# Six chunks, the first weights and the first block in a computed order; a norm with two matmuls; a tile-wise end

## The chip, the cores and the metric

One core of one Trainium2 chip. The metric is the device time of one execution in microseconds (us). TensorE (PE) multiplies, VectorE (DVE) does elementwise work, ScalarE (ACT) activations and copies, GpSimd (POOL) and SyncE (SP) issue DMAs. Every engine runs its own instructions in order, and waits on semaphores of the others.

## The reference

A gated linear recurrence over 768 steps in 32 heads, and then two gated MLPs with weights of their own, the second behind an RMS norm:

```
for t in range(S):                                   # S = 768, head_dim D = 48
    state = alpha[:, :, t, :, None] * state + outer(k[:, :, t], v[:, :, t])
    y[:, :, t] = q[:, :, t] @ state
x  = y, as [B * S, H * D]                            # 3072 tokens x 384
x  = (silu(x @ w_gate) * (x @ w_val)) @ w_out        # d_ff = 1536
xn = x / sqrt(mean(x * x) + 1e-6) * rms_g
out = (silu(xn @ w_gate2) * (xn @ w_val2)) @ w_out2
```

## The kernel before

The recurrence is cut into 24 chunks of 128 steps (6 for each of 4 batches, batch by batch in turn), 8 heads at a time as four pairs. Within a chunk it goes by levels b = 1, 2, 4, ... 64. `start_chunk` multiplies q by alpha (DVE). `products` (DVE) multiplies neighbouring alphas, `merge` (DVE) multiplies them into q and k in place, and `copy_qk` (ACT) copies q and k of a level out before the next merge overwrites them. `scores` (PE) multiplies the copies, `masks` (DVE) and `copies_p` (ACT) bring the scores out of PSUM, and `outputs` (PE) multiplies them with v into the tile Y. `kv` and `state` carry the state on, `turn` of k (L479) is a transpose that `kv` needs, and `split_x` (ACT, then DVE) brings Y out as x, in a high and a low part. The first six chunks start from level 1 and take the diagonal on DVE (`direct_ops`); the later ones start from level 4, with a longer `direct_ops`.

The MLPs run over blocks of 3 or 4 chunks (seven in the first layer, six in the second). Each block goes over 12 slices f of d_ff: three (block 0) or nine matmuls into g, the same into v, `s = silu(g) * v` (ACT, DVE), and an output group `o` one f later. Block 0 of the first layer, written (0,0), uses the weights in plain fp32 as `conv` has put them together from raw words (ACT and DVE; tiles `room` and `x`); the other blocks use weights split into a high and a low part (`split_hi`, `split_lo`) and x so split too, which takes three matmuls for one.

The order of the instructions is the order in which the program is written out. `chunk(n, T)` issues what chunk n does in slot T, and a chunk begins every 12 slots (NS). `run` first issues the 44 slots up to `UNTIL[0]`, with a step of `conv` every fifth slot (PRE); these hold chunks 0 to 2 and the first slots of chunk 3. Then it goes over the MLP's points (three for each f), and after each of them issues a share of the slots that belong to the block: chunks 3 to 5 and the first eight slots of chunk 6 beside block (0,0), chunks 6 to 8 beside (0,1), and so on. Weight loads go out on POOL's queue, all others on SP's. vl, vn and dir (v by level, v, and the operands of `direct_ops`) have one buffer, qk and its alpha two.

The second layer needs the norm of each block, `norm_steps`, issued step by step beside the block before. It sums squares over partitions with four matmuls that have one column each (L571), works on columns of 4, and spreads the result with four matmuls of 128 columns (L590). The last three output tiles go out through `evac`: copy (ACT) into one of two tiles `ev`, and a store from SP.

## Time and profile before

| | us |
|---|---|
| median of 3 runs (1121.33 to 1121.57) | 1121.56 |
| the profiled execution | 1124.23 |
| its span, first to last instruction | 1122.5 |
| PE busy in the span | 1066.4 (95%) |
| DVE busy | 655.1 (58%) |
| ACT busy | 415.8 (37%) |

The profile is of one execution. A matmul in plain fp32 shows as two records there (x6 for three matmuls). Busy times are sums of instruction durations, and instructions that follow each other closely overlap a little. A name on the left of an arrow is written, on the right read; L651 is a line of the kernel above. "Idle before" is the time that an engine stood still ahead of an instruction, with what released it.

### The profile page before, as it was taken

To read this page: it belongs to the slowest core of one execution; us is meant where nothing else is said; L and a number is where in the kernel's file an instruction comes from. 1 tells how busy PE (TensorE), PEld (TensorE's weight loads), DVE (VectorE), ACT (ScalarE), POOL (GpSimd) and SP (SyncE) were. 2 spreads that over 40 slices of the span, in tenths; PEclk is the share of its full clock that TensorE was granted. 3 is DMA by queue.
4 is the path that set the end of the run, shared out by engine and by line. 5 is a ranking of instruction groups with operands and counts; after the bars stand their busy time and mean duration, and the time that the engine had idled before them with its cause. 6 is when DMAs were issued, how large, how long until landed. Compare 5 with 4: busy or idle time off the path is not lost.

```text
span 1122.5 us, 25564 instructions
## 1 busy us (share of the span) xinstructions
PE 1066.4 (95%) x10944; PEld 887.4 (79%) x10944; DVE 655.1 (58%) x1361; ACT 415.8 (37%) x770; POOL 45.6 (4%) x81
## 2 busy tenths in 40 slices
PE   2668999999999999999999999999999999999997
PEld 2545669999999878878888888888888888888886
DVE  4779966887778877767737777723323324233221
ACT  3465624543344433333425444331232322322222
POOL 2012000000000000000000000000000000000000
PEclk9889999999999999999999999999999999999999
DMA  8657524443464443444324343010000100100000
GB/s 259 181 175 235 157 80 128 114 119 97 109 152 135 125 135 103 120 122 113 96 81 173 127 141 127 16 41 1 29 29 1 48 10 1 57 1 1 29 1 29
DMA packets 56018, 103.64 MB, mean 92 GB/s; under 512 B 7392, under 2 KB 40672, under 8 KB 55904
## 3 DMA queue, kind: packets, MB, share of 16 engines
q1 hardware_dynamic: 50592, 80.37, 24.7%
q0 software_dynamic: 5312, 21.63, 5.7%
q8 instruction: 86, 1.41, 0.5%
...
## 4 chain that ended last, share of the span: by engine, by line
PE 85%; DVE 2%; DMA 2%; ACT 1%; issue 1%; SPq 0%; ACTq 0%; DVEq 0%; POOLq 0%
PE g L651 25%; PE o L692 25%; PE v L651 25%; PE Y L340 4%; PE Y L297 3%; DMA x2d<-ev 1%; PE Y L380 1%; PE Y L335 1%; PE Y L479 1%; PE Y L590 0%; DMA ydd<-yd 0%; PE Y L571 0%; DVE qk L230 0%; DMA room<-w 0%; ACT ev L612 0%
## 5 line engine op out<-in xcount | busy, mean ns | idle before, releaser
L661 DVE TENSOR_TENSOR s<-s,v 128x512 f32<-128x512 f32 (+1 forms) x156 | 100.6, 645 | 315.4 <-PE v L651 314.5
L651 PE MATMUL g<-xhi,w 128*128 128x512 f32 (+1 forms) x864 | 280.5, 379 | 0.0
L651 PE MATMUL v<-xhi,w 128*128 128x512 f32 (+1 forms) x864 | 280.2, 378 | 0.0
L692 PE MATMUL o<-hh,w 128*128 128x512 f32 (+1 forms) x864 | 208.6, 376 | 0.0
L658 ACT ACTIVATE s<-g 128x512 f32<-128x512 f32 (+1 forms) x156 | 88.0, 564 | 270.6 <-PE g L651 238.9
L667 ACT ACTIVATE hh<-s 128x512 fp32r<-128x512 f32 (+1 forms) x144 | 87.2, 606 | 270.6 <-DVE s L661 270.5
L651 PEld LDWEIGHTS g<-xhi,w 128*128 128x128 f32 x864 | 161.2, 188 | 27.1
L651 PEld LDWEIGHTS v<-xhi,w 128*128 128x128 f32 x864 | 161.2, 188 | 26.1
L692 PEld LDWEIGHTS o<-hh,w 128*128 128x128 f32 x864 | 159.8, 188 | 26.1
L651 PE MATMUL g<-xlo,w 128*128 128x512 f32 (+1 forms) x432 | 163.2, 378 | 2.5 <-DVE xlo L411 2.5
L651 PE MATMUL v<-xlo,w 128*128 128x512 f32 (+1 forms) x432 | 162.4, 376 | 0.0
L692 PE MATMUL o<-hl,w 128*128 128x512 f32 (+1 forms) x432 | 122.0, 389 | 1.7 <-ACT ev L612 1.5
L673 DVE TENSOR_TENSOR hl<-s,hh 128x512 fp32r<-128x512 f32 (+1 forms) x144 | 94.2, 654 | 45.4 <-ACT hh L667 37.2
L651 PEld LDWEIGHTS g<-xlo,w 128*128 128x128 f32 x432 | 81.1, 188 | 17.0 <-DVE xlo L411 4.3
L651 PEld LDWEIGHTS v<-xlo,w 128*128 128x128 f32 x432 | 81.2, 188 | 12.5
L692 PEld LDWEIGHTS o<-hl,w 128*128 128x128 f32 x432 | 76.9, 188 | 17.3 <-ACT ev L612 2.5
L230 DVE TENSOR_TENSOR qk<-qk,bpb 128x512 f32<-128x512 f32 x96 | 65.9, 687 | 25.8 <-PE Y L297 15.3
L253 ACT ACTIVATE kc<-qk 128x512 f32<-128x512 f32 x72 | 45.5, 631 | 47.5 <-DVE qk L230 47.2
L340 PE MATMUL Y<-pt,vl 64*32 64x64 f32 (+1 forms) x2880 | 48.3, 228 | 3.4 <-issue 2.1
L340 PEld LDWEIGHTS Y<-pt,vl 64*32 64x32 f32 (+1 forms) x2880 | 41.3, 110 | 10.7 <-issue 7.5
L230 DVE TENSOR_TENSOR qk<-qk,bpa 128x512 f32<-128x512 f32 x48 | 32.9, 686 | 4.5 <-ACT px L253 2.8
L318 DVE TENSOR_TENSOR pt<-Y,mask 128x256 f32<-128x256 f32 x63 | 23.4, 417 | 15.8 <-ACT pt L329 15.8
...
## 6 DMA issues: line engine op xcount, KB each, us to landing
...
```

Of the source, the lines that this page charges most:

```text
L230: self.nc.vector.tensor_tensor(out=v, in0=v, in1=sub(t, o, [(1, 2), (2, nb), (0, b)]), op=ALU.mult)
L253: self.nc.scalar.activation(out=sub(t, 0, [(NP * 64, 2), (b, NP * 64 // b), (1, b)]), in_=v, func=AF.Copy)
L297: self.nc.tensor.matmul(out=sc[o:o + w, p] if l < 3 else sc[o:o + w, p // 2, p % 2], lhsT=kc[d, p, gs], rhs=qc[d, p, gs], start=True, stop ...
L318: self.nc.vector.tensor_tensor(out=p, in0=sc, in1=m, op=ALU.mult)
L335: self.nc.tensor.matmul(out=self.Y[:, k, 0:C], lhsT=yn[:, C * k:C * k + C], rhs=self.ident, is_transpose=True, start=True, stop=False, ski ...
L340: mm = lambda o, a, x: self.nc.tensor.matmul(out=o, lhsT=a, rhs=x, start=False, stop=False, skip_group_check=True)
L651: nc.tensor.matmul(out=ps[:, :N], lhsT=a, rhs=x, start=(q == 0), stop=(q == len(ops) - 1))
L658: nc.scalar.activation(out=s[:, :N], in_=g[:, :N], func=AF.Silu)
L661: nc.vector.tensor_tensor(out=s[:, :N], in0=s[:, :N], in1=v[:, :N], op=ALU.mult)
L667: nc.scalar.activation(out=hh[:, :N], in_=s[:, :N], func=AF.Copy)
L673: nc.vector.tensor_tensor(out=hl[:, :N], in0=s[:, :N], in1=hh[:, :N], op=ALU.subtract)
L692: nc.tensor.matmul(out=O[gj][i][:, :N], lhsT=a[:, 128 * i:128 * i + 128], rhs=x[:, :N], start=(f == 0 and q == 0), stop=(f == NF - 1 and q ...
```

## The change

Before the second block there are no slots any more. `plan_chunk` (chunks 0 to 5, BEGIN), `plan_weights`, `plan_mlp` (block 0) and `plan_split` hand every step to a list scheduler, `Plan`, with its engine, a duration, what it reads and writes, and a due time. `Plan.order` repeatedly looks, on each engine, at the steps whose inputs are there, takes those that could begin within 0.3 us of the earliest, and of these the one that is due first; the steps are issued by the start times that come out. Odd chunks get second buffers for vl, vn and dir (`vlo`, `vno`, `diro`) in tiles that are free so early. Chunk 0's second half and the zero fill of its tile go out on ACT's queue, a first activation stands ahead of them for its table, and the loads of weights 1 and 2 wait until chunks 0 and 1 have made some copies (`gate`). Block (0,1) now has 44 slots beside it (all of chunk 6 to 8).

The norm squares and adds as before, splits the sum into a high and a low part, and multiplies both with a 128 x 128 matrix of ones, so that every partition gets the sum of every token; the rest goes over 128 x 512 instead of 128 x 4, and the four matmuls of L590 fall away. The last output piece goes tile by tile, high parts first, each tile has a place of its own in SBUF, the third goes in halves, and ACT and DVE share the copies.

```diff
-PRE = 0.2
-CONV1, CONV2 = 1.34, 1.0
+CONV2 = 1.0
+AHEAD, RATE = 0.3, 280.0
+ARRIVE = ((7.0, (("qk", 0), ("al", 0))), (10.0, (("dir", 0),)), (14.0, (("hi", 0), ("lo", 0))))
 EXTRA = 2
+BEGIN = 6
+START, SPAN, PIECE, LEAD = 50.0, 29.0, 7.3, 11.0
...
+class Plan:
+
+
...
+    def add(self, engine, us, fn, reads=(), writes=(), due=0.0, size=0):
+        reads = [t for t in reads if t not in writes]
+        need = set()
+        for t in reads:
+            need |= self.last.get(t, set())
+        for t in writes:
+            need |= self.last.get(t, set()) | self.seen.get(t, set())
...
+    def order(self):
+
+        free, end, got, wire = {}, {}, [], 0.0
+        todo = list(range(len(self.ops)))
+        while todo:
+            ready = {}
+            for i in todo:
+                engine, us, _, need, due, _ = self.ops[i]
+                if all(j in end for j in need):
+                    t = free.get(engine, 0.0)
+                    for j in need:
+                        t = max(t, end[j] + (0.0 if self.ops[j][0] == engine and not self.ops[j][5] else self.sem))
+                    ready.setdefault(engine, []).append((t, due, i))
+            best = None
+            for engine, c in ready.items():
+                first = min(c)[0]
+                pick = min((x for x in c if x[0] <= first + self.ahead), key=lambda x: (x[1], x[0], x[2]))
+                if best is None or pick[0] < best[0]:
+                    best = pick
+            t, _, i = best
+            engine, us, _, _, _, size = self.ops[i]
+            free[engine] = end[i] = t + us
+            if size:
+                wire = max(wire, t + us) + size / self.rate
+                end[i] = wire + 1.8
+            todo.remove(i)
+            got.append((t, i))
+        self.times = got, end
+        return [self.ops[i][2] for _, i in sorted(got)]
...
+    def other(self, n):
+        return n < BEGIN and n % 2
+
+    def vl(self, n, l):
+        return self.vlo[l] if self.other(n) else self.vlt[l]
 
     def load_vn(self, n):
-        t = self.vnt[n] = self.a1.tile([128, NP, 2, D], F32, tag="vn", name="vn")
+        t = self.vnt[n] = self.vno if self.other(n) else self.a1.tile([128, NP, 2, D], F32, tag="vn", name="vn")
...
+    def plan_chunk(self, n):
+
+        add, i, early = self.plan.add, n % 2, self.early(n)
+        qk, al, vn, dr = ("qk", i), ("al", i), ("vn", i), ("dir", i)
+        t0, w = (9 + LEAD * n, 1.3) if early else (START + SPAN * (n - 3), SPAN / 20)
+        due = lambda x: t0 + w * x
+        bp = lambda b: al if b == 1 else ("bp", b, i)
...
+        if n:
+            add("SP", .8, lambda: self.load_qk(n), (), (qk, al), due(-9), 590)
+        if n:
+            add("SP", .4, lambda: self.load_vn(n), (), (vn,), due(-2), 196)
+            add("SP", .8, lambda: (self.load_dir(n, 0), self.load_dir(n, 1)), (), (dr,), due(-3), 393)
...
+        add("DVE", .61, lambda: self.start_chunk(n), (al,), (qk, "bpa", ("bpb", i)), due(0))
+        for l, b in enumerate(LEVELS):
+            if b < 64:
+                add("ACT", .58, lambda l=l: self.copy_qk(n, l), (qk,), (al,) if b == 32 else (("kc", l),), due(l))
+            if b == 1:
+                add("DVE", .35, lambda: self.products(n, 1), (al, "bpa"), (bp(2),), due(.5))
+            if b == 64:
+                break
+            add("DVE", .61, lambda b=b: self.merge(n, b), (bp(b), *bpt(b)), (qk,), due(l + 1))
+            add("DVE", (.21, .14, .1, .09, .08, .08)[l], lambda b=b: self.products(n, 2 * b),
+                (bp(2 * b), *bpt(2 * b), *bpt(4 * b)), (bp(4 * b),), due(l + 1.1))
...
+        if early:
+            for ls in ((0, 1), (2,), (3, 4), (5, 6)):
+                score(ls, due(max(ls)))
+        else:
+            score(tuple(range(NL)), due(7))
+        add("DVE", .61, lambda: self.merge(n, 64), (bp(64), ("bpb", i)), (qk,), due(8.5))
...
+        add("ACT", 1.14, lambda: step(0), (hi,), (w,), due)
+        add("ACT", 1.2, lambda: step(1), (), (lo,), due + .1)
+        add("DVE", .66, lambda: step(2), (), (w,), due + 1)
+        add("DVE", 1.28, lambda: step(3), (lo,), (w,), due + 2)
+        add("DVE", 1.28, lambda: step(4), (hi,), (w,), due + 3)
...
+        add("PE", 1.94, lambda: gv("g", 0), (("W", f), *xs), ("g",), due)
+        add("ACT", .45, silu, ("g",), (s,), 0)
+        add("PE", 1.94, lambda: gv("v", 1), (("W", f), *xs), ("v",), due + 1)
+        add("DVE", .48, mult, ("v",), (s,), 0)
+        if f < NF - 1:
+            add("PE", 1.94, lambda: self.out_piece((0, 0), f, T["s"], self.W32[0, f], self.O), (("W", f), s), ("o0", "o1", "o2"), due + 3)
...
-        ss = self.Y[:, 0, 0:MB]
-        for c in range(MB):
-            nc.tensor.matmul(out=ss[:, c:c + 1], lhsT=q0[:, c * C:(c + 1) * C], rhs=self.ones[:, 0:1], start=True, stop=True,
-                             skip_group_check=True)
-        yield
-        a, r, t = (self.n1.tile([128, MB], F32, tag=t, name=t) for t in ("msq", "rstd", "tmpn"))
+        hl = [self.n1.tile([128, NW], F32R, tag=t, name=t) for t in ("sqh", "sql")]
+        nc.scalar.activation(out=hl[0], in_=q0, func=AF.Copy)
+        yield
+        tt(out=hl[1], in0=q0, in1=hl[0], op=ALU.subtract)
+        yield
+        ss = self.Y[:, 0]
+        for i in range(2):
+            nc.tensor.matmul(out=ss, lhsT=self.ones, rhs=hl[i], start=(i == 0), stop=(i == 1))
+        yield
+        a, r, t = self.n1.tile([128, NW], F32, tag="msq", name="msq"), q0, q1
         nc.vector.tensor_scalar(out=a, in0=ss, scalar1=1.0 / DM, scalar2=EPS, op0=ALU.mult, op1=ALU.add)
+        yield
         nc.vector.tensor_scalar(out=t.bitcast(I32), in0=a.bitcast(I32), scalar1=1, scalar2=None, op0=ALU.logical_shift_right)
         nc.vector.tensor_scalar(out=r.bitcast(I32), in0=t.bitcast(I32), scalar1=-1, scalar2=0x5F3759DF, op0=ALU.mult, op1=ALU.add)
         for _ in range(3):
             yield
             tt(out=t, in0=r, in1=r, op=ALU.mult)
+            yield
             stt(out=t, in0=t, scalar=-0.5, in1=a, op0=ALU.mult, op1=ALU.mult)
+            yield
             stt(out=r, in0=t, scalar=1.5, in1=r, op0=ALU.add, op1=ALU.mult)
-        yield
-        for c in range(MB):
-            nc.vector.tensor_scalar(out=q0[:, c * C:(c + 1) * C], in0=self.ident, scalar1=r[:, c:c + 1], scalar2=None, op0=ALU.mult)
-        yield
-        rb = self.Y[:, 1]
-        for c in range(MB):
-            o = slice(c * C, (c + 1) * C)
-            nc.tensor.matmul(out=rb[:, o], lhsT=self.ones, rhs=q0[:, o], start=True, stop=True, skip_group_check=True)
         yield
...
-                stt(out=x[:, k], in0=x[:, k], scalar=self.g2[:, k:k + 1], in1=rb, op0=ALU.mult, op1=ALU.mult)
+                stt(out=x[:, k], in0=x[:, k], scalar=self.g2[:, k:k + 1], in1=r, op0=ALU.mult, op1=ALU.mult)
...
-    NORM = 13 + KT + 1
+    NORM = 20 + KT + 1
...
+    def last_piece(self, ops, o):
+
+        nc = self.nc
+        N, c0 = MB * C, (NCH - MB) * C
+        cols = [(0, slice(0, N)), (1, slice(0, N)), (2, slice(0, N // 2)), (2, slice(N // 2, N))]
+        t = [self.n1.tile([128, NW], F32, tag=f"sq{i % 2}", name="ev") if i else self.rp.tile([128, NW], F32, tag="ev", name="ev", bufs=2)
+             for i in range(KT)]
+        for i in range(KT):
+            for q, (a, x) in enumerate(ops):
+                nc.tensor.matmul(out=o[i][:, :N], lhsT=a[:, 128 * i:128 * i + 128], rhs=x[:, :N], start=False,
+                                 stop=(q == len(ops) - 1))
+        for n, (i, c) in enumerate(cols):
+            if n % 2:
+                nc.vector.tensor_copy(out=t[i][:, c], in_=o[i][:, c])
+            else:
+                nc.scalar.activation(out=t[i][:, c], in_=o[i][:, c], func=AF.Copy)
+            (nc.scalar if n == 3 else nc.sync).dma_start(
+                out=self.d["out"][128 * i:128 * i + 128, c0 + c.start:c0 + c.stop], in_=t[i][:, c])
...
+        half(nc.sync, 0, 0)
+        half(nc.scalar, 0, 1)
+        pad(nc.scalar, 0, 0)
+        pad(nc.scalar, 0, 1)
+        warm = self.const.tile([128, 1], F32, name="warm")
+        nc.vector.memset(warm, 0.0)
+        nc.scalar.activation(out=warm, in_=warm, func=AF.Silu)
...
+        for n in range(BEGIN):
+            self.plan_chunk(n)
+            if n < 2:
+                held = self.kcx[0][:, 0, 0, 0:1]
+                plan.add("POOL", .2, lambda n=n, a=held: nc.gpsimd.tensor_copy(out=gate[:, n:n + 1], in_=a),
+                         (("kc", 0), ("kc", 3)), ("gate",), 0)
+                plan.add("POOL", 1.6, lambda n=n: self.raw_at(n + 1), ("gate",), (("hi", n + 1), ("lo", n + 1)), 0, 1180)
...
+        for f in range(NF):
+            self.plan_weights(f)
+            self.plan_mlp(f)
+        for f in range(BEGIN):
+            self.plan_split(f)
+        for fn in plan.order():
+            fn()
...
-                    side, total = (self.slot(i) for i in range(UNTIL[j], UNTIL[j + 1])), UNTIL[j + 1] - UNTIL[j]
+                    a = UNTIL[j] if j > 1 else NS * (BEGIN - 1)
+                    side, total = (self.slot(i) for i in range(a, UNTIL[j + 1])), UNTIL[j + 1] - a
```

On DVE, at the end of chunk 0's levels (qk_88 is the tile of even chunks, qk_89 that of odd ones; the last number is the level b). Before:

```order
L222 TENSOR_TENSOR bpb<-bpb 128x4
L318 TENSOR_TENSOR px<-early,mask 128x256 x2
L318 TENSOR_TENSOR pt<-early,mask 128x256
L421 TENSOR_TENSOR dir<-dir 128x384
L318 TENSOR_TENSOR pt<-early,mask 128x256
L431 TENSOR_REDUCE dir<-dir 128x8
L429 TENSOR_TENSOR yn<-vn,dir 128x384
L158 TENSOR_SCALAR x_118<-x_118 128x1152
L318 TENSOR_TENSOR pt<-early,mask 128x256
L230 TENSOR_TENSOR qk_88<-qk_88,bpb 128x2x4x64
L239 TENSOR_TENSOR qk_89<-qk_89 128x512
```

and now:

```order
L273 TENSOR_TENSOR qk_88<-qk_88,bpb 128x2x32x8
L465 TENSOR_TENSOR yn<-vn,dir 128x384
L273 TENSOR_TENSOR qk_88<-qk_88,bpb 128x2x16x16
L357 TENSOR_TENSOR px<-early,mask 128x256 x2
L273 TENSOR_TENSOR qk_88<-qk_88,bpb 128x2x8x32
L280 TENSOR_TENSOR qk_89<-qk_89 128x512
L357 TENSOR_TENSOR pt<-early,mask 128x256 x2
L265 TENSOR_TENSOR bpa<-qk_89 128x256
L273 TENSOR_TENSOR qk_88<-qk_88,bpb 128x2x4x64
L357 TENSOR_TENSOR pt<-early,mask 128x256
L273 TENSOR_TENSOR qk_89<-qk_89 128x2x256
```

The first product of chunk 1 (qk_89) moved ahead of chunk 0's last merge and two of its masks, and chunk 0's own diagonal moved in between its merges.

On PE, at the start of block 0 (x_118 and x_121 hold weights 0 and 1, x_119 and x_122 weights 2 and 3). Before:

```order
L651 MATMUL g<-x_417,x_118 128x384 x3
L651 MATMUL v<-x_417,x_118 128x384 x3
L297 MATMUL Y<-px 32x32 x32
L297 MATMUL Y<-kc 64x64 x24
L297 MATMUL Y<-qk_89 64x64 x16
L651 MATMUL g<-x_417,x_118 128x384 x3
L651 MATMUL v<-x_417,x_118 128x384 x3
L479 MATMUL Y<-ident,qk_89 128x128 x4
L692 MATMUL o_1080<-s,x_118 128x384
L692 MATMUL o_1081<-s,x_118 128x384
```

and now:

```order
L654 MATMUL g<-x_504,x_121 128x384 x3
L654 MATMUL v<-x_504,x_121 128x384 x3
L654 MATMUL g<-x_504,x_121 128x384 x3
L872 MATMUL o_961<-s,x_121 128x384
L872 MATMUL o_962<-s,x_121 128x384
L872 MATMUL o_963<-s,x_121 128x384
L654 MATMUL v<-x_504,x_121 128x384 x3
L654 MATMUL g<-x_504,x_122 128x384 x3
L336 MATMUL Y<-px 32x32 x32
L336 MATMUL Y<-kc 64x64 x24
```

Chunk 3's scores (Y) moved behind the first g of weight 2, and an output group stands two groups behind the v that it depends on.

On PE in the second layer, at the norm. Before, the first of the two places:

```order
L651 MATMUL v<-xhi,w 128x512 x2
L651 MATMUL v<-xlo,w 128x512
L651 MATMUL v<-xhi,w 128x512
L571 MATMUL Y<-ones,sq_8043 128x1 x4
L692 MATMUL o_7999<-hl,w 128x512
```

and now:

```order
L872 MATMUL o_7997<-hh,w 128x512
L872 MATMUL o_7998<-hh,w 128x512
L768 MATMUL Y<-sqh,ones 128x512
L768 MATMUL Y<-sql,ones 128x512
L834 MATMUL g<-xhi,w 128x512
```

The second place (L590, four matmuls) is gone.

## Rows read from the trace of the kernel before

**Rows 1.** The page's busy tenths of 40 equal slices; PEclk is the granted clock.

```profile
PE   2668999999999999999999999999999999999997
...
DVE  4779966887778877767737777723323324233221
...
PEclk9889999999999999999999999999999999999999
```

**Rows 2.** By stretch: length, busy PE, PEld, DVE, ACT, POOL; clock, DMA share, GB/s.

```profile
0.00:69.50 69.50, 31.39 (x1053) 27.36 (x1053) 40.64 (x89) 29.60 (x51) 10.54 (x24) 0.90 0.77 220
69.50:165.80 96.30, 89.98 (x1310) 56.83 (x1311) 82.46 (x138) 53.55 (x83) 11.66 (x21) 0.98 0.51 158
165.80:239.90 74.10, 73.67 (x1112) 69.15 (x1111) 59.07 (x142) 34.18 (x74) 3.91 (x6) 1.00 0.39 112
```

**Rows 3.** DVE's waits up to 69.5: total us, times, longest.

```profile
DVE qk L239 <- DMA qk<-zero: 8.6, 1, 8.6
DVE qk L230 <- ACT px L253: 8.2, 8, 2.3
DVE qk L230 <- ACT kc L253: 4.1, 7, 0.6
DVE dir L421 <- DMA dir<-qn: 2.2, 1, 2.2
...
DVE qk L230 <- ACT qk L253: 1.5, 2, 0.9
```

**Rows 4.** DVE in time order: start us, us, instruction, [idle before].

```profile
9.65 0.69 DVE L239 TENSOR_TENSOR qk<-qk 128x512 f32<-128x512 f32 x1 [8.65 <-DMA qk<-zero]
...
11.69 0.69 DVE L230 TENSOR_TENSOR qk<-qk 128x512 f32<-128x512 f32 x1 [1.01 <-ACT px L253]
...
18.96 0.69 DVE L230 TENSOR_TENSOR qk<-qk,bpb 128x512 f32<-128x512 f32 x1 [0.92 <-ACT qk L253]
...
26.36 0.68 DVE L239 TENSOR_TENSOR qk<-qk 128x512 f32<-128x512 f32 x1
```

**Rows 5.** SP in time order, its first loads.

```profile
0.74 1.79 SPq L94 DMA_DIRECT2D qk<-qka  x4
```

**Rows 6.** Tile qk up to 12 us: its transfers, from issue to landing.

```profile
DMA to landing us min/median/max: 4.1/7.5/9.7
```

**Rows 7.** PE in time order, block 0, and the first matmul of the second.

```profile
69.53 3.90 PE L651 MATMUL g<-x,x 128*128 128x384 f32 x6 [3.96 <-ACT x L405]
...
129.28 2.10 PE L651 MATMUL g<-x,x 128*128 128x384 f32 x6
...
159.31 2.10 PE L651 MATMUL g<-x,x 128*128 128x384 f32 x6
...
165.83 0.63 PE L651 MATMUL g<-xhi,w 128*128 128x384 f32 x1
```

**Rows 8.** PE in time order, around the norm's matmuls of one block.

```profile
690.26 0.95 PE L571 MATMUL Y<-ones,sq 128*128 128x1 f32 x8
691.08 0.94 PE L692 MATMUL o<-hl,w 128*128 128x512 f32 x3
...
713.62 1.06 PE L590 MATMUL Y<-sq,ones 128*128 128x128 f32 x8
714.43 0.48 PE L651 MATMUL v<-xhi,w 128*128 128x512 f32 x1
```

**Rows 9.** The chain that ended last: start us, us; a group of nine.

```profile
598.42 2.04 PE g L651 x9
```

**Rows 10.** PE and ACT in time order, the end of the span.

```profile
1113.90 0.96 PE L692 MATMUL o<-hl,w 128*128 128x512 f32 x3 [0.20 <-DVE hl L673]
...
1114.70 1.53 PE L692 MATMUL o<-hh,w 128*128 128x512 f32 x6
...
1118.55 0.60 ACT L612 ACTIVATE ev<-o 128x512 f32<-128x512 f32 x1 [1.65 <-DMA out<-ev]
```

398 lines of the change are left out of this document (238 added, 160 removed).

## The prediction

> **What bounds the kernel now.** I read the busy tenths first [rows 1]. From about a tenth of the span on, PE stands at 9 in nearly every slice, and its granted clock is full: there the kernel is bound by PE, and only PE work taken out of it, or a wait of PE's, shortens it. The first slices are different. PE is at 2 to 8 and DVE at 4 to 9. So the second view is the busy time by stretch [rows 2], cut at the first matmul of the first block (69.5 us) and at the first of the second block (165.8). Up to 69.5 the three early chunks are made; DVE is busy for 40.64 us of it and idle for 28.9, and PE for less than half. From 69.5 to 165.8 the first block runs; PE is at 90 of 96.3. From 165.8 on PE has no room (73.67 of 74.1).
>
> Why DVE idles early is the third view [rows 3]: 8.6 us for the first load, 2.2 us for a later one, and 8.2 + 4.1 + 1.5 = 13.8 us for ScalarE's copies. The rows of one chunk show how [rows 4]: before each of the six merges of a level DVE waits for the copy of the level before, 1.01 us the first time and 0.92 the last, 4.2 us in sum over the six. Nothing else is there to run, since the next chunk's first product comes only at 26.36, when this chunk is through. The early part is a chain of latencies, one chunk after the other.
>
> **Step 1: when the first block can start.** The change puts the next chunk's product right behind the sixth merge, and gives odd chunks buffers of their own, so that two chunks are under way at once. DVE's work up to the first block hardly changes: by the order, 22 merges instead of 25 stand ahead of it, the rest nearly cancels, so 40.6 - 3 x 0.69 = 38.5 us. The first product now runs at 9.65, released by a zero fill that POOL issued. In the change these fills and half of chunk 0's load go out on ScalarE's queue. The transfers into this tile took 4.1 to 9.7 us to land [rows 6], so the product could run between 4.9 and 9.65; I take 7.0, nearer to the middle, since the fills stand behind the half load. Of the 28.9 us of idle time 9.5 lie ahead of the first product and 19.4 behind it. All of these would stay if the copies hold every chunk up as before, none if the second chunk always has something ready. I keep 5: the 4.2 of the first chunk, which is still alone for its six merges, and a little at the end of chunk 2. That gives 7.0 + 38.5 + 5 = 50.5 for the first matmul of block 0, against 69.53; the ends are 7.0 + 38.5 = 45.5 and 65.
>
> One rule speaks against the 7.0. In the rows the four loads of the tile kept SP's queue for 1.79 us [rows 5], and the fills came from POOL. The Trainium skill (DMA: Bandwidth & Descriptors, section "Issuing engines are not separate DMA queues") says that transfers started by several engines run interleaved on the same 16 DMA engines, so that a second issuing engine saves the issue time alone. By that rule the product would come some 1.3 us earlier, at 8.4, and the sum would be 1091.4 instead of 1090. The spread of 4.1 to 9.7 us for one tile is what I go by; the rule's value lies inside my range.
>
> **Step 2: the first block.** Where nothing waits, four f of block 0 with one chunk take from 129.28 to 159.31, 30.0 us [rows 7]. Twelve f with three chunks are 90.1, less one output group of 2.1 that falls into the next block: 88.0. Now the stage takes 165.83 - 69.53 = 96.3, so 8.3 are lost, 1.8 of them to the half clock at its start (3.90 us for six matmuls, 2.10 later). The planner's order keeps the same groups. DVE's 82.46 us there [rows 2] lose chunk 6's share (11, step 3), and 71 fit beside 88. It leaves some places tight (an output group stands right behind the product that it needs), and PE comes from a sparse stretch as before. I take 4.5: the 1.8 again and 2.7 of waits; the ends are 0 and the 8.3 of now. So the second block starts at 50.5 + 88.0 + 4.5 = 143.0: 22.8 us earlier.
>
> **Step 3: the second block.** The whole of chunk 6 now runs beside block 1, 44 slots instead of 36. These eight slots are DVE and ScalarE work. At 59.07 us for 36 slots [rows 2] they cost at most 13.1; I take 11, since the MLP's own products in the 59 don't grow, and 1 for one more weight split. DVE then has 71 of 74.1 us. PE's work is the same, so this is hidden if the waits of DVE, 15 us now, shrink to 3. PE never stands still for long there, so these are waits of an engine that keeps to PE's pace, and they shrink when it has more to do. I charge 1 us; the ends are 0 and 12.
>
> **Step 4: the norm.** Its matmuls stand in PE's full stretch. The four of one column hold the stream from 690.26 to 691.08, the four of the spread-out row from 713.62 to 714.43: 0.82 + 0.81 us a block [rows 8]. Nine matmuls of 128x512 take 2.04 [rows 9], so the two new ones take 0.45. That is 1.18 a block and 7.1 for six. DVE's part grows from columns of 4 to rows of 512: nine steps at no more than the 0.69 of a product of that size, 6 us a block. This lies beside PE, with DVE at 2 or 3 tenths from two thirds of the span on [rows 1]. If the new operand came late by one DVE instruction (0.69) each time, 4.1 would go; its subtraction stands an output group ahead of its use, so I take 7.1, with 3.0 as the other end.
>
> **Step 5: the end.** Now the third evacuation waits for the first tile's store: it runs at 1118.55 to 1119.15 [rows 10], and the span ends 3.35 later. The last matmul ends at 1114.70 + 1.53 = 1116.23, after a wait of 0.20 for the low part, which is now needed later. With a third tile and halves on two engines the last evacuation ends about 0.4 (two thirds of the 0.60) behind that, at 1116.4, less the 0.2: 1116.2, and the span 3.35 later: 2.9 us less. Ends 2.0 (the fourth store queues) and 3.2 (the half evacuation takes 0.3 and its start gains too).
>
> **Sum.** 22.8 - 1.0 + 7.1 + 2.9 = 31.8. The profiled execution took 1124.23 with a span of 1122.5; it would take 1092.4. The median of the runs lies 2.7 below it, so 1089.8: **1090**.
>
> **Rivals.** First, *the early part stays a chain*. The merges wait for the copies, the copies share ScalarE with the weights' steps, which the new order puts between them, and a plan can't shorten an instruction. Then all 19.4 us stay, the block starts at 65, and the time is 1090 + 14.5 = 1104. For it: 13.8 us of these waits are for ScalarE. Against it: ScalarE is busy for only 29.6 of 69.5 us [rows 2], so the waits are latency, which a second chunk can fill. Chance 0.15.
>
> Second, *DVE becomes the bound beside block 1*: step 3 costs 12 instead of 1, time 1101. For it: 71 of 74.1. Against it: DVE waits there for what comes at PE's pace, and can work ahead of it where it has more to do. Chance 0.10.
>
> Third, on the other side, *loads that come late stop an engine in order*. A chunk's first product needs its load, the load must wait until the buffer's last reader is through, and in the new order this product stands ahead of the last merges of the chunk before: a late load holds up two chunks and the weights behind them. Chunks 2 to 6 have such a load. With 31.8 us to lose, it decides from 6.4 us uncovered at each of the five. At 9.7, the longest landing of that tile [rows 6], with nothing to cover it, it costs 48.5: 1138. Against it: the buffer's last reader, the transpose of k, stands ahead of all but the first merges of the other chunk, so the load has most of a chunk's time to land. Chance 0.05.
>
> **How the numbers follow.** Forecast 1090 with 0.68; 1104 with 0.15; 1101 with 0.10; slower with 0.05; the gains just eaten up, 0.02. Range: low from step 1 at 45.5 and step 2 without loss, 1090 - 5 - 4.5 = 1080; high to the first rival, 1105. Beyond it lies the slow rival, and below it hardly anything, since PE's work can't shrink further. Faster by over 0.2% has 0.93, within 0.2% 0.02, slower 0.05 (0.2% is about what a measurement of this kernel can tell from no change).
>
> **What would show it.** Step 1: first matmul of block 0 near 50, DVE's waits for copies before it down from 13.8 to about 5. Step 2: second block's first matmul near 143, full clock in between, and PE waits of a few us in the stretch. Step 3: block 1 again about 75 us long. Step 4: one pair of matmuls a block, 0.45 us, no wait in front. Step 5: the span ends about 3.7 us behind the last matmul. A block start at 60 or later, or DVE waiting for DMA by more than 10 us after its first product, would prove me wrong.

## The result, and the profile after

The changed kernel takes 1105.29 us (median of 4 runs, 1104.28 to 1109.1) against 1121.57: 0.9857 of the time before (interval 0.983 to 0.9884). The forecast was 1090, with a range up to 1105. The profiled execution took 1104.64, its span is 1102.8. So it is faster by 16 us, where 32 were forecast.

The page's busy tenths, beside those of before [rows 1]; the DMA rows are the busy share of the 16 DMA engines and what they moved.

```profile
PE   4799999999999999999999999999999999999998
...
DVE  5699958977678877767737978834434335344222
...
PEclk9699999999999999999999999999999999999999
DMA  9877213544554544444325343010000100100000
```

By stretch, cut as before [rows 2] (length, busy PE, PEld, DVE, ACT, POOL; clock, DMA share, GB/s); the first row is the opening, then blocks (0,0), (0,1) and (0,2):

```profile
0.00:60.73 60.73, 36.78 (x1054) 27.82 (x1054) 38.65 (x86) 30.36 (x52) 10.19 (x24) 0.83 0.90 249
60.73:151.68 90.95, 88.89 (x1312) 55.97 (x1312) 75.41 (x119) 48.98 (x78) 11.61 (x22) 1.00 0.53 169
151.68:229.81 78.13, 75.61 (x1112) 70.63 (x1111) 67.75 (x161) 37.35 (x79) 3.91 (x6) 0.98 0.38 104
229.81:305.00 75.19, 73.29 (x1115) 69.43 (x1114) 54.47 (x140) 29.38 (x69) 3.90 (x6) 1.00 0.45 117
```

The two spans differ by 19.7 us, and the starts of the blocks say where:

| stretch | before | after | gain | forecast |
|---|---|---|---|---|
| up to block (0,0) | 69.53 | 60.73 | 8.8 | 19.0 |
| block (0,0) | 96.30 | 90.95 | 5.35 | 3.8 |
| block (0,1) | 74.08 | 78.13 | -4.05 | -1.0 |
| block (0,2) | 73.67 | 75.19 | -1.5 | 0 |
| the three blocks behind it | 271.67 | 271.30 | 0.4 | 0 |
| six blocks with the norm of the next beside them | 454.44 | 446.49 | 7.95 | 7.1 |
| the last block and the end | 82.81 | 80.01 | 2.8 | 2.9 |

DVE's waits up to the first block (total us, times, longest), to be read against [rows 3]: ScalarE's copies, 13.8 us before, are down to 1.0. What is left is loads, and x of the chunk before, which a state waits for.

```profile
DVE qk L280 <- DMA qk<-zero: 8.4, 1, 8.4
DVE qk L280 <- DMA qk<-qka: 4.4, 1, 4.4
DVE S L423 <- ACT x L441: 3.9, 2, 1.9
DVE other L457 <- DMA other<-qn: 1.4, 1, 1.4
DVE qk L273 <- ACT kc L292: 1.0, 5, 0.2
```

DVE in time order, the first products of chunks 0, 1 and 2 (start, us, instruction, [idle before]): chunk 1 starts 9 us behind chunk 0, before chunk 0 is through (in [rows 4] it was 16.7), but chunk 2 only 18.9 us behind chunk 1.

```profile
9.47 0.69 DVE L280 TENSOR_TENSOR qk<-qk 128x512 f32<-128x512 f32 x1 [8.44 <-DMA qk<-zero]
...
18.48 0.68 DVE L280 TENSOR_TENSOR qk<-qk 128x512 f32<-128x512 f32 x1
...
37.37 0.69 DVE L280 TENSOR_TENSOR qk<-qk 128x512 f32<-128x512 f32 x1 [4.44 <-DMA qk<-qka]
```

Cut at these products, the same view of the changed kernel shows who was busy meanwhile:

```profile
0.00:9.47 9.47, 0.00 (x0) 0.00 (x0) 0.22 (x2) 1.49 (x2) 3.25 (x10) 1.00 0.85 160
9.47:37.37 27.90, 18.98 (x482) 14.74 (x482) 18.42 (x44) 14.20 (x23) 4.02 (x8) 0.82 1.01 302
37.37:60.73 23.36, 17.80 (x572) 13.08 (x572) 20.00 (x41) 14.67 (x27) 2.92 (x6) 0.78 0.79 223
```

From 9.47 to 37.37 no compute engine is full, but the DMA engines are: 1.01. In the whole opening they are busy for 0.90 x 60.73 = 54.7 us; before, by [rows 2], for 0.77 x 69.5 = 53.5. The forecast start of 50.5 lies below both. This is a warning and no floor, since a busy share is not a fixed amount of work: 0.85 went with 160 GB/s in the first of these stretches, 1.01 with 302 in the second. At 302 GB/s, the highest of the three, the 15.1 MB of the opening (249 GB/s x 60.73 us) would take an estimated 50 us.

Chunk 2's load, which the product at 37.37 waits for, went out late:

```profile
30.84 1.81 SPq L149 DMA_DIRECT2D qk<-qka  x2
```

Of the loads on SP's and ScalarE's queues the ninth to the twenty-eighth (up to 29 us) each went out within 0.9 us behind the landing of the eighth load before it, 16 of the 20 within 0.03. So this program has no more than eight of them under way at a time, and a load that lands late makes those behind it go out late too; the planner does not count with that.

Behind the opening, PE in time order where it stands still in block (0,1), and at the first low part of block (0,2):

```profile
162.80 0.45 PE L872 MATMUL o<-hl,w 128*128 128x384 f32 x1 [2.14 <-ACT ev L803]
...
231.41 0.45 PE L834 MATMUL g<-xlo,w 128*128 128x384 f32 x1 [1.26 <-DVE xlo L447]
```

### The profile page after: what moved, and what is told of

It reads as the page before. It is cut to its first block, busy times and chain, and to the rows that moved or that the text cites. A ratio compares the mean times of both kernels' runs of the same rounds, so it can differ in the third digit from the quotient of the medians.

```text
span 1102.8 us, 25372 instructions
## 1 busy us (share of the span) xinstructions
PE 1064.2 (96%) x10860; PEld 880.1 (80%) x10860; DVE 687.4 (62%) x1346; ACT 417.6 (38%) x776; POOL 45.2 (4%) x81
## 4 chain that ended last, share of the span: by engine, by line
PE 78%; issue 2%; DMA 2%; ACT 1%; DVE 1%; POOL 0%; SPq 0%; ACTq 0%; POOLq 0%; DVEq 0%
PE g L834 24%; PE o L872 24%; PE v L834 24%; PE Y L382 3%; PE Y L336 2%; DMA x2d<-ev 1%; PE Y L416 1%; PE Y L377 1%; DMA yn<-ydd 1%; PE Y L507 0%; DMA ydd<-yd 0%; ACT ev L803 0%; PE Y L768 0%; PE o L888 0%; DVE qk L273 0%
## 5 line engine op out<-in xcount | busy, mean ns | idle before, releaser
L843 DVE TENSOR_TENSOR s<-s,v 128x512 f32<-128x512 f32 (+1 forms) x144 | 94.0, 653 | 275.5 <-PE v L834 275.0
L840 ACT ACTIVATE s<-g 128x512 f32<-128x512 f32 (+1 forms) x144 | 82.1, 570 | 251.3 <-PE g L834 220.7
L292 ACT ACTIVATE kc<-qk 128x512 f32<-128x512 f32 x72 | 45.4, 630 | 38.4 <-DVE qk L273 37.9
L382 PE MATMUL Y<-pt,vl 64*32 64x64 f32 (+1 forms) x2520 | 43.5, 225 | 1.0 <-DMA vl<-vl 1.0
L382 PEld LDWEIGHTS Y<-pt,vl 64*32 64x32 f32 (+1 forms) x2520 | 35.4, 108 | 9.2 <-issue 5.8
```

Of the source, the lines that this page charges most:

```text
L292: self.nc.scalar.activation(out=sub(t, 0, [(NP * 64, 2), (b, NP * 64 // b), (1, b)]), in_=v, func=AF.Copy)
L382: mm = lambda o, a, x: self.nc.tensor.matmul(out=o, lhsT=a, rhs=x, start=False, stop=False, skip_group_check=True)
L840: nc.scalar.activation(out=s[:, :N], in_=g[:, :N], func=AF.Silu)
L843: nc.vector.tensor_tensor(out=s[:, :N], in0=s[:, :N], in1=v[:, :N], op=ALU.mult)
```

## The experiments

Each is compared with the kernel before on the same chip (1123.7 to 1124.7 us there), so ratios are compared. Each kernel but e15_shift has four runs or five; the lengths come from one of them. "Start" is the first matmul of block (0,0) in the profiled execution, then the lengths of the first blocks.

| kernel | ratio to before (interval) | start | (0,0) | (0,1) | (0,2) |
|---|---|---|---|---|---|
| before | 1 | 69.53 | 96.30 | 74.08 | 73.67 |
| the change | 0.9857 (0.983, 0.9884) | 60.73 | 90.95 | 78.13 | 75.19 |
| e12_again (the change once more) | 0.9861 (0.984, 0.9883) | 62.24 | 92.07 | 76.90 | 75.08 |
| e1_order | 0.9829 (0.9812, 0.9846) | 59.89 | 92.66 | 78.34 | 75.19 |
| e2_gates | 0.9815 (0.9798, 0.9831) | 59.67 | 91.87 | 78.68 | 75.08 |
| e3_evac | 0.984 (0.9826, 0.9855) | 62.54 | 91.51 | 78.82 | 72.66 |
| e4_late | 0.9905 (0.989, 0.992) | 68.44 | 96.12 | 74.05 | 73.62 |
| e5_bytes | 0.9871 (0.9846, 0.9896) | 62.24 | 95.22 | 78.48 | 75.03 |
| e6_twice | 0.9879 (0.9863, 0.9896) | 66.48 | 92.42 | 78.55 | 75.08 |
| e7_slots | 0.9807 (0.9792, 0.9822) | 63.50 | 92.06 | 74.40 | 73.75 |
| e8_one | 0.9957 (0.9943, 0.9971) | 71.52 | 96.72 | 78.39 | 74.87 |
| e9_novl | 0.9804 (0.9789, 0.9819) | 56.56 | 91.98 | 76.91 | 75.05 |
| e10_first | 0.9875 (0.9852, 0.9898) | 65.16 | 91.42 | 78.34 | 75.03 |
| e11_both | 0.979 (0.9773, 0.9806) | 60.82 | 92.07 | 74.38 | 73.82 |
| e13_wide | 0.9832 (0.9815, 0.9848) | 59.52 | 91.24 | 76.80 | 75.03 |
| e14_best | 0.9804 (0.9786, 0.9823) | 58.71 | 94.04 | 74.38 | 73.60 |
| e15_shift | 0.9884 (one run, no interval) | 62.57 | 96.39 | 76.93 | 74.97 |

Four of them (the change, e12_again, e3_evac, e7_slots) have the same opening and start between 60.73 and 63.50. So one trace alone tells nothing about a start that moves by less than some 3 us.

### The two late parts alone

**e4_late**: the kernel before with the new `norm_steps` and `last_piece`.

```diff
-    NORM = 13 + KT + 1
+    NORM = 20 + KT + 1
...
+        if (gj, f) == (ORDER[-1], NF - 1):
+            self.last_piece(ops[1:] + ops[:1], O.pop(gj))
+            return
```

> The kernel before with the two late parts of the change alone: the norm with two matmuls and the tile-wise end. By the block lengths of the two traces (75.67 against 74.34 us a block in the second layer, 7.95 for the six; 82.81 against 80.01 for the last block) these are worth 10.75 us, so 1121.6 becomes 1110.8 (1110 to 1112). If the late parts drew on the early ones (a cooler start, other loads), less than 9 or more than 12.5 us would come out.

1113.33 against 1124.37, 11.0 us; the blocks of the second layer take 74.34, as in the change. Steps 4 and 5 stand by themselves, and the rest of the change brings some 5 us of 16.

### Block (0,1): order, or too much for DVE

**e3_evac**

```diff
-            want = total * pt // (3 * NF - (4 if nj >= 0 else 0))
+            want = total * pt // (3 * NF - (4 if nj >= 0 else 2 if gj == (0, 1) else 0))
+            if piece < 2:
+                self.evac()
             while done < min(want, total):
...
-            if piece < 2:
-                self.evac()
```

> The changed kernel, with two moves in the order of blocks (0,1) and later: at a point of the MLP the evacuation of the block before is issued ahead of the side slots of that point (before: behind them), and the 44 slots of block (0,1) are spread over 34 points instead of 36. No work is added or taken away. Theory 'ACT in order': the 2.14 us that PE lost at 162.8 come from the third evacuation, which stood behind two of chunk 6's copies, and these waited for merges; the 1.26 us at 231.4 from the low part of x, whose split stood in the last slots. Then both waits go, the half clock behind the first one too, block (0,1) takes 74 to 75 us instead of 78.13 and (0,2) 73.7 to 74 instead of 75.19; the time falls by 4 to 5 us. Theory 'DVE is the bound' (the second rival of the prediction): DVE was busy for 67.75 of the 78.13, the waits come back at other places, and (0,1) stays at 77 or more.

Little of it came. Block (0,2) lost its wait for xlo (72.66), and the wait for the evacuation fell to 1.13, but block (0,1) stayed at 78.82: PE now waited there 1.49 for an xlo, 0.94 for an hl and 0.58 for a mask, all of them DVE's. The two blocks together took 151.5 us, against 153.3 in the change and 152.0 in its repetition. This order alone didn't help an engine that is behind.

**e7_slots**

```diff
+        for T in range(8):
+            plan.add("DVE", 1.4, lambda T=T: self.slot(NS * (BEGIN - 1) + T), (), (("qk", 0), ("al", 0), ("dir", 0), "bpa", ("bpb", 0), ("kc", T)),
+                     118 + 2.5 * T)
...
-                    a = UNTIL[j] if j > 1 else NS * (BEGIN - 1)
+                    a = UNTIL[j]
```

> The changed kernel, with chunk 6's first eight slots given to the planner as well (eight steps of 1.4 us on DVE, due late), so that block (0,1) has 36 slots beside it, as before the change. Theory 'DVE is the bound' (second rival of the prediction): the 11 us of DVE work taken out of block (0,1) are what made it 78.13 instead of 74.1; it goes back to 74 to 74.5, the 2.14 us wait for the third evacuation and the half clock behind it go, and block (0,0), where DVE was busy for 75.4 of 91, grows by at most 2 to 3. The time falls by 2 to 4 us. Theory 'order alone': the evacuation still stands behind chunk 6's work, and the block stays at 77 or more.

By stretch, blocks (0,0), (0,1) and (0,2) of this kernel (columns as above):

```profile
63.50:155.56 92.06, 88.88 (x1311) 55.91 (x1312) 85.07 (x145) 51.36 (x82) 11.64 (x22) 1.00 0.52 166
155.56:229.96 74.40, 73.61 (x1112) 69.14 (x1111) 59.27 (x139) 34.80 (x75) 3.92 (x6) 1.00 0.40 111
229.96:303.71 73.75, 73.10 (x1115) 69.32 (x1114) 53.12 (x136) 29.75 (x70) 3.91 (x6) 1.00 0.45 115
```

With DVE at 59.27 instead of 67.75 us, block (0,1) is back at 74.40 and (0,2) at 73.75; of the two waits 0.7 us for an evacuation, in (0,2), are left. Block (0,0) took the work (DVE 85.07 of 92.06) and is no longer than in the repetition of the change. So the eight slots were too much for this block, and they had room one block earlier. They hold ScalarE's work too, which the edit does not tell apart; but ScalarE was busy for only 37.35 of the 78.13 us, and PE's waits in e3_evac were for DVE.

### The opening: loads, or a chain of copies

**e1_order** and **e2_gates** move one load forward, or bytes back.

```diff
-            add("SP", .4, lambda l=l: self.load_vl(n, l), (), (("vl", l, i),), due(2 + l), 131)
+            add("SP", .4, lambda l=l: self.load_vl(n, l), ("kt",) if n == 1 else (), (("vl", l, i),), due(2 + l), 131)
```

> The changed kernel, with one thing moved: the planner holds chunk 1's seven v loads back until chunk 0's transpose of k has been copied, so that chunk 2's load of q, k and alpha stands ahead of them on SP's queue. Bytes, DVE work and copies are as they were. Theory 'late load': in the changed kernel this load was issued at 30.84 and landed at 37.4, while its buffer had been free since about 21.8, and DVE stood still for 4.44 us in front of chunk 2. Then it is issued at about 24, DVE's wait for it goes, and the first matmul of block 0 comes at 56 to 57 instead of 60.73; the time falls by about 4 us, to 1101. Theory 'chain of copies' (the first rival of the prediction): the wait only changes its name, DVE waits for copies or scores instead, and the first matmul stays at 60 to 61.

```diff
-        self.raw_at(0)
...
-            if n < 2:
+            if n < 3:
...
-                plan.add("POOL", 1.6, lambda n=n: self.raw_at(n + 1), ("gate",), (("hi", n + 1), ("lo", n + 1)), 0, 1180)
+                plan.add("POOL", 1.6, lambda n=n: self.raw_at(n), ("gate",), (("hi", n), ("lo", n)), 0, 1180)
```

> The changed kernel, with the raw words of the first three weights loaded one chunk later each: weight 0 when chunk 0 has made its first copies (before: at once, 2.42 us), weight 1 after chunk 1's (before: chunk 0's), weight 2 after chunk 2's (before: chunk 1's). The same bytes in all, but 1.18 MB less ahead of chunk 0's first product and ahead of each of the next two chunks. Theory 'bytes': the DMA engines stood at a busy share of 0.85 to 1.05 from the start to 37 us, so what is loaded early delays what is needed early; the first product comes at 7 to 8.5 instead of 9.47, chunk 2's load lands 3 to 6 us earlier, and the first matmul of block 0 comes at 54 to 57 instead of 60.73. Theory 'SP's order': the loads stand in SP's queue one behind the other whatever else is moved, chunk 2's load lands less than 2 us earlier and block 0 starts at 59 or later. Theory 'chain of copies': 60 to 61, with waits for copies.

Neither gave what it should. In e1_order SP issued chunk 2's load 5.6 us earlier than in the change (25.28 instead of 30.84); the product that waits for it came 1.3 us earlier:

```profile
36.04 0.69 DVE L280 TENSOR_TENSOR qk<-qk 128x512 f32<-128x512 f32 x1 [2.16 <-DMA qk<-qka]
```

The load was under way for 10.8 us instead of 6.5: it took its place among the others. In e2_gates the product ran at 35.24. Both starts are below the scatter by some 1 us; in time e2_gates is some 5 us ahead of the change and e1_order 3, which is at the edge of the intervals. The first product did not move in e2_gates (9.92).

**e6_twice** and **e9_novl** add bytes and take them away, with the order of the compute engines unchanged.

```diff
-                plan.add("POOL", 1.6, lambda n=n: self.raw_at(n + 1), ("gate",), (("hi", n + 1), ("lo", n + 1)), 0, 1180)
+                plan.add("POOL", 1.6, lambda n=n: [self.raw_at(n + 1) for _ in range(2 - n)], ("gate",), (("hi", n + 1), ("lo", n + 1)), 0, 1180)
```

> The changed kernel, with the raw words of weight 1 loaded twice into the same place, one after the other (1.18 MB more on POOL's queue, from about 12 to 30 us; nothing reads the first copy). Theory 'bytes': at the 320 to 350 GB/s of that stretch they cost 3.4 to 3.7 us of the DMA engines ahead of chunk 2's load, which lands at 39 to 41 instead of 37.4; block 0 starts at 63 to 65 instead of 60.73 and the time grows by 2 to 4 us. Theory 'something else holds chunk 2': no more than 1 us of difference at the start of block 0.

```diff
-        return self.vlo[l] if self.other(n) else self.vlt[l]
+        return self.vlt[l]
...
-            add("SP", .4, lambda l=l: self.load_vl(n, l), (), (("vl", l, i),), due(2 + l), 131)
+            add("SP", .4, lambda l=l: None if n else self.load_vl(n, l), (), (("vl", l, i),), due(2 + l), 131)
```

> The changed kernel without the v loads by level of chunks 1 to 5 (35 loads of 131 KB, 14 of them for chunks 1 and 2): those chunks are computed with chunk 0's v, so the output is another. Every other instruction stands where it stood. Theory 'the DMA engines are the bound of the opening' (busy for 0.90 of the 60.73 us ahead of block 0): with 1.8 MB less for chunks 1 and 2 chunk 2's load lands at 30 to 33, DVE's wait of 4.4 us for it goes, PE waits for no v, and block 0 starts at 54 to 57. Theory 'the chain of PE, ACT and DVE': chunk 0's x, which stood at 32.05 in the change and at 32.0 where the load was earlier, and the states behind it hold chunk 2 all the same, and block 0 starts at 59 or later.

Chunk 2's product in e6_twice:

```profile
41.81 0.69 DVE L280 TENSOR_TENSOR qk<-qk 128x512 f32<-128x512 f32 x1 [6.28 <-DMA qk<-qka]
```

and in e9_novl:

```profile
35.48 0.69 DVE L280 TENSOR_TENSOR qk<-qk 128x512 f32<-128x512 f32 x1 [1.48 <-DMA qk<-qka]
```

In e6_twice the load went out at 30.01, no later than in the change, and was under way for 11.8 us instead of 6.5: 1.18 MB more on another queue held it up, so the loads share the DMA engines. The block started 3 to 6 us later than in the kernels with the same opening. But the profiled execution was the slowest of this kernel's four (1113.18; the others 1109.3 to 1109.9), and in time its interval overlaps that of the change.

e9_novl, in which chunks 1 to 5 are computed with chunk 0's v, started 5.7 us earlier than the repetition in the same set, and took 0.57% less time. It takes away more than bytes: with fewer loads in SP's queue, chunk 2's load went out nearly 6 us earlier than in the change,

```profile
24.99 0.79 SPq L149 DMA_DIRECT2D qk<-qka  x2
```

as it does in e1_order, which moves all the bytes (25.28). It landed at nearly the same time in both (35.45 and 35.94), later than I expected (30 to 33). The larger part of the gain lies behind it: chunk 1's state followed after 10.9 us (46.38), in e12_again after 13.4 (38.10 to 51.51) and in e1_order after 11.4. What e9_novl has over e1_order at the start, 3.3 us, comes with 2.7 us less of stops of PE, which are described below, and in time the intervals of the two overlap. So that loads delay each other is shown; that the bytes alone set the length of the opening is not.

**e10_first** holds everything back until chunk 0's q, k, alpha and fill are there.

```diff
         for h in range(2):
+            p = slice(64 * h + 32, 64 * h + 64)
+            nc.gpsimd.tensor_copy(out=self.ident[p, 0:1], in_=self.qk[0][p, 0, 0, 0:1])
+        self.load(self.ident, self.ident_d)
+        for h in range(2):
             pad(nc.gpsimd, 1, h)
...
```

> The changed kernel, with everything that is loaded held back until q, k, alpha and the zero fill of chunk 0 are there: two one-column copies on POOL read them and write into the place of the identity, which SP loads first now; mask, diagonal, v, chunk 1 and the raw words of weight 0 stand behind. Taking weight 0's words alone away from the front did not help (the fill's wait was 8.9 us instead of 8.4). Theory 'the opening transfers share the DMA engines': with nothing beside them the two halves and the fills land after 4 to 5 us, as the shortest transfer into that tile did (4.1), and the first product comes at 5.5 to 7 instead of 9.47; what is held back then comes 2 to 4 us later, so that chunk 0's diagonal waits, and block 0 starts between 59 and 62. Theory 'the fill has its own latency': the first product stays at 9 or later, and block 0 comes at 63 or later.

The first products, and the diagonal that had to wait, in time order on DVE:

```profile
6.60 0.69 DVE L280 TENSOR_TENSOR qk<-qk 128x512 f32<-128x512 f32 x1 [5.56 <-POOL ident L937]
...
15.30 0.56 DVE L457 TENSOR_TENSOR dir<-dir 128x384 f32<-128x384 f32 x1 [5.10 <-DMA dir<-qn]
```

So the fill alone lands in time for 6.60, and what holds it at 9.47 are the transfers beside it. But the 2.9 us won are paid back more than once: 5.10 for the diagonal, and the block starts at 65.16, not between 59 and 62.

**e5_bytes** has the order of e1_order and the raw words two chunks later.

```diff
-            if n < 2:
+            if n in (1, 2):
...
+                plan.add("POOL", 1.6, lambda n=n: self.raw_at(n - 1), ("gate",), (("hi", n - 1), ("lo", n - 1)), 0, 1180)
+            if n == 2:
+                plan.add("POOL", .2, lambda: nc.gpsimd.tensor_copy(out=gate[:, 0:1], in_=self.Sc[1][:, 0, 0:1]),
+                         (("S", 1),), ("gate",), 0)
+                plan.add("POOL", 1.6, lambda: self.raw_at(2), ("gate",), (("hi", 2), ("lo", 2)), 0, 1180)
```

> The changed kernel, with chunk 2's load ahead of chunk 1's v loads in SP's queue, and the raw words of the first three weights two chunks later than in the change: weight 0 when chunk 1 has made its first copies (about 20 us), weight 1 after chunk 2's, weight 2 when chunk 1's state is there. So 2.4 MB less ahead of chunk 2's load than in the change. Moving the load ahead alone had it issued at 25.3 and landed at 36.0 (10.8 us under way), the first later gates 25.5 and 35.2. Theory 'bytes': the load is now under way for 4 to 6 us and lands at 28 to 31, DVE waits for no load after its first product, and block 0 starts at 54 to 57. Theory 'something else holds chunk 2': the load lands before 32, but the start stays at 59 or later, and the waits in front of the states and merges (for ACT and PE) grow instead; the late weights would then show as waits of ACT for raw words.

DVE did not wait for chunk 2's load any more, yet it started chunk 2 at 33.39 and block 0 at 62.24: my theory failed here. It now waited 9.6 us for x of the chunks before, and in block (0,0) PE waited 3.7 us for a weight that came late. So loads are not the only thing that holds the opening. PE in time order shows what else there is:

```profile
24.10 0.67 PE L336 MATMUL early<-kc 64*64 64x64 f32 x15
29.23 0.37 PE L336 MATMUL early<-kc 64*64 64x64 f32 x1 [4.46 <-issue]
```

Between the 15th and the 16th of equal matmuls PE stands still for 4.46 us, and waits for nothing that the profile shows; later again for 4.85. Chunk 0's x came behind the first stop, and chunk 2 behind that. All kernels here have a stop at the first of these places: 1.54 us in the change, 2.14 in the kernel before. The long stop is not a later end: PE came to the place at 24.77 here and at 27.75 in the change, went on at 29.23 and 29.29, and chunk 0's x followed at 32.00 and 32.05.

**e15_shift** puts 24 matmuls on a zero tile ahead of everything on PE (48 records in the trace).

```diff
         nc.vector.memset(self.Sd, 0.0)
+        for _ in range(24):
+            nc.tensor.matmul(out=self.Y[0:32, 0, 480:512], lhsT=self.Sd[:, 0], rhs=self.Sd[:, 1], start=True, stop=True,
+                             skip_group_check=True)
```

> The changed kernel, with 24 small matmuls on a zero tile ahead of everything on PE, which stands still there anyway until 10.9 us; their result is never read. In the trace PE stands still twice ahead of block 0 in the middle of a row of equal matmuls, waiting for nothing that the profile shows: after 355 and 734 matmul records in the kernel before, after 356 and about 745 in the changed one and its repetition, for 1.5 to 2.2 us each (up to 4.9 in the kernels with loads brought forward). Theory 'the next piece of PE's program comes late': the place hangs on the number of instructions alone, so with 48 more records in front the first stop comes after 356 records of which 48 are the new ones, that is some 48 records earlier in the old row (not within chunk 1's scores of level 16 but before them), and the second likewise. Theory 'something that these matmuls use is late': the stops stay at the old matmuls, after 404 and 793 records. The start of block 0 stays within 60 to 64 either way.

```profile
24.16 0.75 PE L336 MATMUL early<-px 64*32 64x32 f32 x55
27.36 0.34 PE L336 MATMUL early<-px 64*32 64x32 f32 x9 [2.44 <-issue]
```

The first stop came after 350 matmul records in the change and here, the 48 new ones included, and the second after 732 in both. (The 356 and 745 of the expectation are not counts of matmul records alone.) So the place hangs on the count of instructions. The traces show more. Counted together with PE's weight loads, the stops of over 0.3 us without a releaser, 59 in the 17 traces, all stand at steps of 256 records, give or take one: after 706, 961, 1217, 1473 and so on. And each ends 1.2 to 1.9 us after a packet of 16 KB has landed on the queue that the profile names "instruction": at 27.87 for the stop that ends at 29.29 in the change, at 27.64 for 29.23 in e5_bytes, at 26.06 for 27.36 here. So PE stands still because the next piece of its program comes late. These packets go over the DMA engines too; that the loads make them late is not shown: e6_twice, with more bytes, has a first stop of 1.36 us, and the kernel before, with a DMA share of 0.77, one of 2.14.

Block 0 started at 62.57 in this one execution, and block (0,0) took 96.39: two more such stops in it took 4.7 us.

**e13_wide** moves the same bytes in rows of 2 and 3 KB instead of 1 KB.

```diff
-        for l in range(NL):
-            add("SP", .4, lambda l=l: self.load_vl(n, l), (), (("vl", l, i),), due(2 + l), 131)
+        for ls in GROUPS:
+            add("SP", .4, lambda ls=ls: self.load_vls(n, ls), (), tuple(("vl", l, i) for l in ls), due(2 + ls[0]), 131 * len(ls))
```

> The changed kernel, with the v loads by level of chunks 0 to 5 made in three transfers instead of seven, of levels (0,1), (2,3) and (4,5,6): rows of 2 and 3 KB for each partition instead of 1 KB (their source is laid out so), the same bytes, and 16 loads instead of 28 in SP's queue for a pair of chunks. Theory 'bytes': nothing is taken away, and block 0 starts at 60 to 63 as before. Theory 'packets': the stretches in which 1 KB rows run move 230 to 260 GB/s at a busy share of 0.95, those with raw words 320 to 400, so the same bytes take a quarter less of the DMA engines; chunk 2's load lands at 32 to 35, and block 0 starts at 57.5 to 59.5. If the queue of eight loads under way is what holds SP, the load is issued at 24 to 27 instead of 30.8 but is under way for 8 us or more.

In the first 60 us of e13_wide (packets of all queues; then packets, MB and share of the 16 engines of SP's queue):

```profile
DMA packets 5912, 15.13 MB, mean 252 GB/s; under 512 B 870, under 2 KB 2918, under 8 KB 5903
...
q1 hardware_dynamic: 4751, 9.59, 63.8%
```

and of e12_again:

```profile
DMA packets 8255, 14.66 MB, mean 244 GB/s; under 512 B 1120, under 2 KB 7008, under 8 KB 8245
...
q1 hardware_dynamic: 7093, 9.11, 60.5%
```

A third fewer packets, and the same share for the same bytes: 15.0 MB per 100% here, 15.1 there. Bytes count here, not packets. Nor was the limit of eight loads under way all that held it: with fewer, larger loads chunk 2's went out at 25.15, and landed at 37.5 all the same.

**e8_one** takes the second buffers away.

```diff
     def other(self, n):
-        return n < BEGIN and n % 2
+        return False
...
-        qk, al, vn, dr = ("qk", i), ("al", i), ("vn", i), ("dir", i)
+        qk, al, vn, dr = ("qk", i), ("al", i), ("vn", 0), ("dir", 0)
...
```

> The changed kernel without the second buffers for odd chunks: all chunks share one vl, vn and dir again, and the planner knows it. By the reason given for the change, a chunk's small loads then wait until the chunk before has been through, and two chunks are no longer under way at once: block 0 starts at 66 to 70 (69.5 before the change) and the time is 1111 to 1115. If the DMA engines' bytes set the start, the buffers matter little, since the loads could not have come sooner: block 0 starts at 60 to 63.

71.52, later than the kernel before and than either theory had it: with one buffer the planner's order gains nothing ahead of block 0. So the opening's gain needs the second buffers, which let two chunks be under way.

**e11_both** (slots and gates) and **e14_best** (these and wide rows) are the versions that came out of this.

> Two of the experiments together: chunk 6's first eight slots in the planner, and the raw words of the first three weights one chunk later each. By the first, block (0,1) takes 74.4 instead of 78.13 and (0,2) 73.75 instead of 75.19, 5.2 us less; by the second the start came 1.1 us earlier (59.67), with 0.9 us more in block (0,0). If both hold, the time is 5 us below that of the changed kernel of the same set, some 0.981 of the kernel before; if the second was within the scatter of the opening, it is as with the slots alone (0.9807).

> Three of the experiments together: chunk 6's first eight slots in the planner, the raw words of the first three weights one chunk later, and the v loads in wide rows. The first two gave 0.979 of the kernel before. By 'packets' the start of block 0 comes 2 to 4 us earlier again, 57 to 58.5, and the time is 0.9755 to 0.978; by 'bytes' it stays at 0.979.

e11_both takes 1100.98 beside 1107.87 for the change in the same set, 0.979 of the kernel before. That is the lowest ratio here, but its interval overlaps that of the slots alone (0.9807), so the gates' part is not shown. e14_best started earliest of those with all loads (58.71) and was no faster: its stops of PE in the opening were longer (9.7 us in all), and in block (0,0) (94.04) PE waited 2.7 us for DVE's masks, where it waited 1.1 in the repetition of the change.

**e12_again** is the change once more.

> The changed kernel unaltered, beside the others of this set: on its first chip block 0 started at 60.73 and the time was 0.9857 of that before. In two experiments that left the opening as it is the start came at 62.54 and 63.50, with chunk 2's load landing at 39.2 and 38.8 instead of 37.4. Every theory expects the same here: a start between 60 and 64 and 0.983 to 0.988 of the time before; it tells how far the opening moves by itself.

It fell inside what was expected: start 62.24, 0.9861.

## Why the prediction was wrong, step by step

It stood 15.5 us too low. 12.1 of this are in the span (1102.8 instead of 1090.7). 3.4 come from the last line of the sum: I took off the 2.7 by which the profiled execution of before stood above its median, but that of after stood 0.65 below its own. One execution can stand on either side of a median, and I had no reason to carry the difference over.

**Step 1 failed: 60.73 instead of 50.5.** Its three terms were 7.0 for the first product, 38.5 of DVE's work and 5 of waits. The work was right (38.4 from 9.47 on). The first product came at 9.47, and the waits behind it were 12.8, of which 5.8 are for loads and 3.9 for x of the chunk before. I had counted what waits for what on DVE and ACT, and let every load behind the first product land in time: a term that I put at nothing. The row that speaks against it stood in [rows 2], and I read past it: a DMA share of 0.77 over 69.5 us is 53.5 us, more than the whole opening that I forecast. e6_twice and e10_first show that loads hold each other up there. I also left out that PE stops for the next piece of its program, which the trace of before shows (2.14 and 2.60 us) and behind which chunk 0's x comes.

The 7.0 failed because the transfers beside it slow the first load: the fills on ScalarE's queue brought the product 0.18 us earlier, not 2.6, and with nothing beside them it came at 6.60 (e10_first). The rule of the Trainium skill that I went against (DMA: Bandwidth & Descriptors, section "Issuing engines are not separate DMA queues") has transfers of several issuing engines interleave on the same DMA engines, and this trace agrees. The 8.4 that I had worked out by it was still 1.1 too early.

**The first rival** named 1104 and so came near in time, by luck and not by its mechanism: waits for copies fell from 13.8 to 1.0 us. **The third** had the mechanism, a late load in front of a chunk's first product, at one of five places and at 4.4 us, below the 6.4 at which it would have decided. Against it I had said that the load has most of a chunk's time to land; but it first had to wait for its turn in SP's queue, until 30.84.

**Step 2 was mis-sized on the good side: 2.95 us lost instead of 4.5.** The half clock that I carried over did not come: the granted clock of the stretch was 1.00.

**Step 3 failed: 4.05 in block (0,1) and 1.5 in (0,2) instead of 1.** I had DVE at 71 us (it was 67.75) and took its waits to shrink from 15 to 3. They shrank to 10.4. They are not all of one kind: chunk 6's levels now began with the block, DVE stood still for 0.7 us in all from 152.7 to 167, the third evacuation stood behind two of chunk 6's copies on ACT, and PE stopped for 2.14. Behind this stop the granted clock was 0.61 from 164 to 168 us. In e12_again it stayed at 1.00 behind the same stop (2.13 us, up to 165.45), and the block was 1.2 us shorter. Stretches of 4 us, first of the change, then of e12_again:

```profile
164.00:168.00 4.00, 4.00 (x17) 4.00 (x16) 3.13 (x7) 0.82 (x2) 0.00 (x0) 0.61 0.05 15
```

```profile
168.00:172.00 4.00, 4.00 (x37) 3.75 (x38) 2.86 (x6) 1.02 (x2) 0.42 (x1) 1.00 0.01 2
```

The second rival, to which I gave 0.10, was the case, as e7_slots shows; of its 12 us 5.6 came.

**Step 4 was right**: a pair of matmuls a block, without a wait in front, 0.46 us long (forecast 0.45); 1.34 a block instead of 1.18.

```profile
601.65 0.39 PE L768 MATMUL Y<-sqh,ones 128*128 128x512 f32 x1
601.88 0.39 PE L768 MATMUL Y<-sql,ones 128*128 128x512 f32 x1
602.11 0.39 PE L834 MATMUL g<-xhi,w 128*128 128x512 f32 x1
```

**Step 5 was right**, 2.8 for 2.9. ACT's last evacuations, which wait for PE alone now and not for a store as in [rows 10]:

```profile
1097.54 0.60 ACT L894 ACTIVATE ev<-o 128x512 f32<-128x512 f32 x1 [1.31 <-PE o L888]
1098.93 0.38 ACT L894 ACTIVATE ev<-o 128x256 f32<-128x256 f32 x1 [0.79 <-PE o L888]
```

The range ended 0.29 us short. It took the first rival as the far end of step 1 alone; step 3's own far end (12) was left to a rival, though both can happen at once, and partly did.

Chunk 0's x came at 31.3 to 33.1 us in all kernels whose opening was only rearranged (e10_first, which holds loads back, aside), and there always 2.3 to 2.8 us behind the end of PE's first stop. Open is when it would come without that stop, which no run took away, and what sets the time at which the piece of program lands.
